# A quarter of the argmax masks as signs and the rows' normalisation on ScalarE, with a new written order

## The chip, the cores and the metric

The kernel runs on one core of a Trainium2 chip. The metric is the device time of one execution in microseconds (us). The engines are TensorE (PE in the profile; PEld is its weight load), VectorE (DVE), ScalarE (ACT), GpSimd (POOL) and SyncE (SP), whose queue issues most transfers.

## What is computed

```python
x  = A_u                                   # 1 x 2048 x 448
xn = layernorm(x)
# A: S4 convolution, N = 256 states per channel
K  = einsum("dn,dnl,dn->dl", C, exp(dt*A*l), dt*B).real      # 448 x 2048
yA = causal_conv(xn, K) + xn * Dskip       # by FFT of length 4096
# B: PEER, 16 heads, 64 x 64 experts, top 1
q  = einsum("nd,dhc->nhc", xn, w_q)        # 2 halves of 256
s1, s2 = q1 @ k1.T, q2 @ k2.T              # 2048 x 16 x 64 each
e  = argmax(s1) * 64 + argmax(s2)
act = gelu(sum(xn * u[e]))                 # per token and head
yB = sum over heads of act * v[e]          # softmax over one entry is 1
out = x + yA + yB
```

## The kernel before, in words

Tokens go in 16 tiles of 128 rows. Four kinds of work run side by side on all engines, and each is cut into steps.

- **Normalisation** (`ln`, two tiles at a time): statistics on DVE (L908, L912), a reciprocal root by three Newton turns on `[128, 2]` tiles (L914 to L919), and the row's normalisation by one DVE instruction per tile (L923), which writes `XN[t][:, 1]`. From it come the transposed tile `xt` (L942, L945), the first transform of the convolution (`u_p`, L723, L726, stored to `vu_d`) and a copy of the rows in memory (`xn_d`).
- **Scores** (`score`, one tile at a time): twelve matmul groups (L960, L969) give four PSUM banks of 8 half-heads x 64 scores, from the ring `s2` of three banks. For each bank DVE takes the maxima (`mx`, L984) and then the mask `eq`, which is 0 where the score is the maximum and 1 elsewhere (L991, `not_equal`). The mask gives the bank back. With all four masks there, DVE subtracts position weights (L999) and takes minima (L1002, L1005), which yields the position of the maximum. Every two tiles the expert numbers are put together (L1021 to L1047) and stored (`ix_st`, L1050).
- **Convolution kernel** (56 batches of 8 channels): exponentials on ACT (L589, L591), phase rows on DVE (L613), sine and cosine on ACT (L628, L631, L634), four products on DVE (L659 to L665, steps `s4_v`), reduction matmuls (L681, `s4_k1`), copies (L689, L692), a transform (L701) and a copy to `VK` (L705, `s4_k4`). After every 16 batches the transform of a chunk of 128 channels is multiplied and transformed back (`cv1` L797, `cv3` L807, `cv5` L829, `cv6` L836), stored (`cv7`, `t_d`), loaded again (`f_l1`, `g_l`) and finished (`f_p`, `g_p` L1176); the last chunk's rows end in L1180 and the store L1188.
- **Experts** (64 groups of 4 gathers): POOL gathers rows of u and v (L1082), DVE makes dot products (`e_d`, L1090), ACT and DVE the gelu (L1097 to L1109), DVE a spread matrix `A` (L1113), PE the weighted sum (`e_p`, L1120), ACT copies it (L1131) and POOL adds it to the output by a transfer.

The order in which steps are written decides the order on every engine's queue. It is a string, `ORDER`: each character names a stream of steps (numbered in the order in which `plan` first adds to them), and the next step of that stream is issued. There is no other scheduler: an engine runs its instructions in the written order and waits on semaphores. Each PSUM bank and buffer ring is given back by a named step. `OPT["SG"]` says how many of a tile's four masks are made by ACT: it is 0 before, and then the branch with `AF.Sign` (L994, L995; eight ACT instructions of 128 x 64) is not used.

Of the kernel before, what the change touches and what calls it, by code (L numbers as in the profile page):

```python
# [172 lines left out]
ORDER = (
    "444447HHHHHHHHHHHHHHHHH4444H4HHHHHHHHHHHHHHHH444MN44444444C7CC676788781222222222222222222211D444D011115EEFCDEFF5CDEFP877"
    "777777II34CDD4EF44444CDCD44379EFEF7J444EKJOWHF6PQPKLCDCDEFJKC8EFD888JEF4444CCDEF4C4K8DDJK4Cuu44EFJKLEFJKDIIPJC9999779777"
    "769777799889D9AALAAAABQQQXXEEFFPQQPQQRRRRRYcccccKMNPPPOPQQQQLWHHHHHHHHHHHHPQQPQQRRRRRRRRRZuZGGGGaZMNPOPWPPbSTTUVvvvQQQQH"
    "HHHHVPQQdeeuPQQRRRRRvdeeMNOWdeeHHHHeeeffJKvvvvvPdPeeQQffJKHHwwHPQPPweeeeccHHHdeQLvHQwxQyxHczeHwwPQwdeezgQRMNHRabzRwxwPcy"
    "x!vvvHHPPRJKzQRcRRzQQPIOWIIIz!vvvwRefRSPHQeefwwxJKQTQyxPwuzTfzQhiabJKXz!LffJKLQRRRfghiRMNPOWPJvvvvveeeeffKJwuwuwxuwyxRzf"
    "ffzKLvghiPHZZdeQzfYH!vvvv#$ghUPQPQQcHHccPwwwxwwyxHQedeeicQHzMNOWjkjkQHzQdeHHRPz!vvvvPPPRRHwRwxwHRHyxRHwzQRHQPHHReedQjzce"
    "eeeRQHz!vvfPQfVvQJwwwueeckjxyxQKJeecQzczcRSTkKLRdeMNOWz!RRedevvvvJfwuwuwxufyxIIcXRPzzz!weeeeePPPTUffffeeVKJKLghQYQQghccc"  # L180
    "HHQwwwxwyxeHHHHPPQcQvvvvvwzcQaZb#$HzHQMNOPWz!vvRiidRPPHwwxwyxHHHVRHHRzzz!eedwHHHIJIQPfRRQPQfKJRRRSffwweedeevvvwuxyTjjTUf"
    "KLghwuvvxzQQePMNOWzz!QQQwuReeeJRPijwuRxyfPxzzz!wffffRHvKJKLweeccvvvvvRvPPeHkkkgd#$cHcQQQPPwwxcVHQQvvfyeedwxzHzHeeQHMNOWd"
    "eeeQPHz!XabHQRwwwxHHHyxZRwPPPRRQzRQQRRhizHz!wRfHjvvvvvvvRQPHIHIHJKwwxPMQyxwzQNOWzSJKLwgefQz!QRwwxPPReefRTTURyxRPzkffegff"
    "fzhidQz!eeQhijkJKffghYuuwuHiePPedVVuvvwwvvvvvvwxwyxHJKLvPQQeedeffjMjHfQQQHNOvP#$ekkzHcHQcHRghdPHcRcHRHzcRz!vvvvHRHRHQeee"
    "eeeeHwwPPHHQQPPMwxweccQRyxwzcedeezQijcQcRRQdNOvwwxz!vvQyxwwuuzJKRPzz!RJSTTURffffVVVVRPQPKLJeeeeeeghIIvK+wuwuwwxRQQfffyxX"
    "PPQJfffiQzfaZbKLPzzQQQwvvkghif!MNORwwvwRjjkkeeexyxRzdPfRRghizPQfPReedezRQRjPQvwvvvwxwyxRSY#!vvvvvvedeQ$zfwwwzTxPPz!vMvve"
    "TQNOvfcQQckyxUVghdPPQczRzVecceeeeeRRezwuwuwuwuPlRQijkRQQ!vvvvcQcffffxyxcPPPllllQzzceedeedeeewQQcXeeez!vvvv#QwwwxRwwwwghm"
    "nmnRRyxRxzRzRz!vvvyxfomnviRwzomllnaZbYzz!vfRomnomnpwwwxwuwufyxffeeefzwughdzzwux$RSoomnmlnccc!TeecyxomomnnTiwzffzdeevvvvv"
    "cqqrzghdeeffff!#pvvoommleeffewiweffeecqqnnewxvvvvghdooUcmyxiczzeedeermccXnnz!vvvYwwwwwxyxzfzdeeewwpoofveewxyxqqzeffezzzm"
    "mlnn!vv!$wuwuoeoccccrjjjkkkghifghjjkkdvvvvwucvewuxyxpffeedijkvzzz!vvvvqfgffffeegaZwwqrhijhibdVV#$+ejewwxwwyxwzzz!vvvvwwe"  # L190
    "eeeffxkdkywwwffgeeefecfccxxzzedhijceedz!v%vvcXyxwuwuzzffzkwueeaZebwuxyYeeefffgd!vvvvxzzhieee&z!v%%vfffff(geedcceedwwwhig"
    "weeejjccc#$xyhijwwwwxzzzkeffkd!vvvveexyxk&ffzzz!vv%vefeefc(gcceedfwwchi&wweedeeaZbjxcYfgewuwukyxzzz(def!vvvvwuwuhijeeeff"
    "kxye&(fffgxzzzefwee!vvvvdcc)v)v)vhijeedeccekwfgdww)vcxyxzzzhijw#!vvvveeffkmmeefewnneomomlnwwwfgfceeedom$ccnomhieedpwwwxy"
    "fcceexXnxyxneeeeqzzz!vvvvwuzzwuz!vYoofaZbfwuqrmmlnonoeeegdeehfffpqwucccccxyxzzzivdeefwmnmn!#$qdeeoowghimnmnlffffgdwweeee"
    "feeefvvvvvvXxomomeedcccwwwwrfpnneedyccXhixzzz!vvvvwxywwwxzzzx!vvvvyeeaZbYoomqqrxzzzefeffnomjghkjjkjkk!vvvvijffgfnopwuwuw"
    "uwueekdfffefhixyeexzzqqrjkffecccghijedewz!%v%edkfgeedww#cchijkwwxyxwwwzzzw!exyeeeffeffgfxzzz!eccccceeedhijvwvvvvvvvweedk"
    "&%(eeafffg&wxyxb$Ywuwuwuwuhijeeee(dezzz!%vvffffffxyv)vkgececceedfhixzzzfeec&(!#vvvv$dewwejwwxywcxzghij)vzz!vkeeefedfkeee"
    "www&(efffXgcccfedvvvchxyxij+cwwYeeffkwdeeeaeebffgdzzz!vvvvwwueehijwuee)v)vkfffgwulccceehijkfwucxyxxcdeedyxffgeeeeXzzz!vv"
    "vvzzwz!vvvvwwhieeejkmeedffffgffcnoeewxcccwmnodecmmlednomnompyxeeYzz#$wwwz!vhiwwweexywnnxzzz!qqreefffghoodvvvvvxyxieffzmm"
    "lnoneeezfofmnzghvmcccciwuwuwuwue!podnxyeeofffqqcvvvvvmnmlnoodeexzghizzwwww!vvveeffeeexwwdwfmmnneecwyxxrpoosleedzmzztml#!"  # L200
    "qqccynefffffxzzzccoedeenojkghieeeffjkjkwww$!slefeeefvvvvvrpqqwxwygffhighiffwsxzzzjkjjkkjkttwwxyxghist!jkzzz!#moommr%pq%q"
    "oomrpqqoo$+*&%()rpqqoorpqqr&%&()&,,,,()()-./-./-.-.//")


class Kernel:
    OPT = dict(UE=8, XX=4, CS=2, ZI=2, MG=4, KT=4, HL=2, SG=0, XR=4, OB=3, XT=1, ST=1)
# [688 lines left out]
    def ln(s, ts):  # L895
        p = s.p
        n = len(ts)
        B = {}
        ld = [s.lnl.get(t) or s.ln_load(t, "ln_ld") for t in ts]

        def st(i, t):
            def f():
                if i == 0:
                    B["mv"] = s.sm.tile([128, n, 2], F32, name="mv", bufs=2)
                    B["bs"] = s.sm.tile([128, n, 6], F32, name="bst", bufs=2)
                    for k in ("v", "y", "q"):
# [8 lines left out]
        ops.append((73, lambda: s.nc.vector.tensor_scalar(B["y"].bitcast(I32), B["v"].bitcast(I32), -0.5, 1597463007.0, op0=ALU.mult, op1=ALU.add)))
        for k in range(3):
            ops.append((73, lambda: s.nc.vector.tensor_mul(B["q"], B["y"], B["y"])))
            ops.append((73, lambda: s.nc.vector.scalar_tensor_tensor(B["q"], B["q"], -0.5, B["v"], op0=ALU.mult, op1=ALU.mult)))
            ops.append((73, lambda: s.nc.vector.scalar_tensor_tensor(B["y"], B["q"], 1.5, B["y"], op0=ALU.add, op1=ALU.mult)))  # L919
        v = p.chain("ln_v", "DVE", ops, deps=[v])  # L920
        for i, t in enumerate(ts):
            def nrm(i=i, t=t):
                s.nc.vector.tensor_scalar(s.XN[t][:, 1], s.XN[t][:, 0], B["mv"][:, i, 0:1], B["y"][:, i:i + 1],  # L923
                                          op0=ALU.subtract, op1=ALU.mult)
# [335 lines left out]
```

## Time and profile before

| | |
|---|---|
| median of 3 runs (lowest, highest) | 822.05 us (821.73, 826.15) |
| profiled execution: its time, its span | 816.38 us, 814.6 us |
| PE busy | 664.8 us (82%) |
| DVE busy | 712.6 us (87%) |
| ACT busy | 512.9 us (63%) |
| POOL busy | 350.1 us (43%) |
| mean granted TensorE clock | 0.907 |
| memory traffic | 212.34 MB, mean 261 GB/s |

The profile is one execution. Its page gives busy times, a strip of the span in 40 slices, the chain of work that ended last, and groups of instructions by line with count, total, mean and the idle time before them. The trace answers by stretch of time, by engine, by line and by wait. An engine's durations overlap a little where instructions follow each other directly, so that a group's busy time can be less than count times mean.

### The profile page before, as it was taken

To read this page: it belongs to the slowest core of one execution; us is meant where nothing else is said; L and a number is where in the kernel's file an instruction comes from. 1 tells how busy PE (TensorE), PEld (TensorE's weight loads), DVE (VectorE), ACT (ScalarE), POOL (GpSimd) and SP (SyncE) were. 2 spreads that over 40 slices of the span, in tenths; PEclk is the share of its full clock that TensorE was granted. 3 is DMA by queue.
4 is the path that set the end of the run, shared out by engine and by line. 5 is a ranking of instruction groups with operands and counts; after the bars stand their busy time and mean duration, and the time that the engine had idled before them with its cause. 6 is when DMAs were issued, how large, how long until landed. Compare 5 with 4: busy or idle time off the path is not lost.

```text
span 814.6 us, 19672 instructions
## 1 busy us (share of the span) xinstructions
PE 664.8 (82%) x7628; PEld 364.7 (45%) x7628; DVE 712.6 (87%) x1751; ACT 512.9 (63%) x931; POOL 350.1 (43%) x303
## 2 busy tenths in 40 slices
PE   1898999899999989999687776767877675688893
PEld 0333334343444334344365553446565343466673
DVE  5697889799999999999989879988898898999940
ACT  0657044646635476465649668987778789887931
POOL 2011042433555433345534645666355657555311
PEclk9999999999999999999989976887979677799997
DMA  9989855785978686687999889989878999889779
GB/s 320 312 317 328 280 180 162 250 258 173 310 219 286 190 259 177 189 249 219 365 313 296 249 270 318 302 289 270 274 222 279 336 290 260 220 249 351 223 181 193
DMA packets 139973, 212.34 MB, mean 261 GB/s; under 512 B 45096, under 2 KB 121896, under 8 KB 139816
## 3 DMA queue, kind: packets, MB, share of 16 engines
q0 software_dynamic: 29120, 124.27, 48.8%
q1 hardware_dynamic: 110760, 86.81, 34.8%
q8 instruction: 60, 0.98, 0.5%
q14 instruction: 33, 0.27, 0.1%
HBM read 181.42 MB, written 33.29 MB: 264 GB/s over the span
## 4 chain that ended last, share of the span: by engine, by line
DVE 33%; PE 31%; ACT 20%; DMA 9%; issue 4%; POOL 1%; SPq 1%; DVEq 0%; ACTq 0%
PE sc L960 8%; DVE ue L1090 7%; DVE ph L613 3%; DMA ue<-in_uv_dram,ig 3%; DVE mg L665 3%; ACT CS L631 3%; PE kp L681 3%; ACT CS L628 3%; PE po L1120 3%; ACT CS L634 3%; DVE zi L661 3%; PE U L797 3%; DVE mx L984 2%; PE ip L829 2%; PE up L723 2%
## 5 line engine op out<-in xcount | busy, mean ns | idle before, releaser
L1082 POOL DMA_INDIRECT ue<-in_uv_dram,ig x256 | 308.6, 1205 | 338.2 <-issue 80.3
L960 PE MATMUL sc<-W,xt 128*128 128x512 f32 x384 | 178.5, 604 | 4.1 <-ACT xt L945 3.5
L1090 DVE SCALAR_TENSOR_TENSOR ue<-ue,xr 128x448 f32<-128x448 f32 x256 | 149.1, 618 | 0.0
L960 PEld LDWEIGHTS sc<-W,xt 128*128 128x128 f32 x384 | 69.4, 190 | 96.1 <-issue 88.5
L681 PE MATMUL kp<-mg 128*32 128x64 f32 x1792 | 65.9, 243 | 31.7 <-DVE mg L665 22.1
L1120 PE MATMUL po<-ue,A 128*32 128x448 f32 x512 | 71.2, 635 | 19.5 <-DVE A L1113 17.8
L589 ACT ACTIVATE mg<-lg 128x512 f32<-128x512 f32 x112 | 61.6, 597 | 20.6 <-PE lg L578 19.9
L681 PEld LDWEIGHTS kp<-mg 128*32 128x32 f32 x1792 | 48.4, 123 | 56.9 <-issue 15.7
L665 DVE TENSOR_TENSOR mg<-mg,CS 128x1024 f32<-128x1024 f32 x56 | 68.1, 1217 | 0.0
L661 DVE TENSOR_TENSOR zi<-mg,CS 128x1024 f32<-128x1024 f32 x56 | 68.1, 1217 | 0.0
L681 PE MATMUL kp<-zi 128*32 128x64 f32 x1792 | 65.4, 240 | 2.8 <-issue 2.8
L628 ACT ACTIVATE CS<-ph 128x1024 f32<-128x1024 int32 x56 | 62.2, 1110 | 6.8 <-DVE ph L613 4.3
L613 DVE CUSTOM_DVE_ANT_0 ph<-st,ph 128x512 uint16<-128x512 uint16 (+2 forms) x84 | 65.1, 775 | 1.2
L634 ACT ACTIVATE CS<-CS,halfpi 128x1024 f32<-128x1024 f32 x56 | 64.3, 1149 | 1.5
L631 ACT ACTIVATE CS<-ph 128x1024 f32<-128x1024 int32 x56 | 62.2, 1111 | 0.0
L578 PE MATMUL lg<-lc,rt 32*128 32x512 f32 x112 | 41.9, 561 | 14.1 <-ACT mg L589 7.1
L797 PE MATMUL U<-VU,g 128*64 128x128 f32 x384 | 44.0, 312 | 11.1 <-ACT tq L836 4.2
L681 PEld LDWEIGHTS kp<-zi 128*32 128x32 f32 x1792 | 50.8, 125 | 0.2 <-issue 0.2
L984 DVE TENSOR_REDUCE mx<-sc 128x8 f32<-128x512 f32 x64 | 43.5, 680 | 7.8 <-PE sc L960 4.2
L829 PE MATMUL ip<-cp,e 64*128 64x256 f32 x384 | 49.0, 410 | 0.0
L701 PE MATMUL vp<-f,kt 128*64 128x128 f32 x448 | 37.3, 299 | 13.8 <-DVE kt L692 12.5
L991 DVE TENSOR_TENSOR eq<-sc,mx 128x512 bf16<-128x512 f32 x64 | 43.6, 682 | 0.7
(244 smaller groups left out, 1184.7 us busy)
## 6 DMA issues: line engine op xcount, KB each, us to landing
wq<-in_wq_dram SPq DMA_DIRECT2D x32, 448.0 KB
xr<-xn_d SPq DMA_DIRECT2D x64, 224.0 KB
vu_d<-vst SPq DMA_DIRECT2D x64, 112.0 KB
VU<-vu_d SPq DMA_DIRECT2D x12, 512.0 KB
t_d<-tq SPq DMA_DIRECT2D x24, 256.0 KB
tl<-t_d SPq DMA_DIRECT2D x12, 512.0 KB
ue<-in_uv_dram,ig POOLq DMA_INDIRECT x256
xx<-in_x_dram SPq DMA_DIRECT2D x16, 224.0 KB
```

What stands on the lines that cost most here:

```text
L613: s.nc.vector.tensor_tensor(out=rw(n, 2 * n), in0=rw(0, n), in1=o["st"][:, k, b0:b0 + 2].rearrange("p b h m x -> p (b h m x)")[:, None].to ...
L628: s.nc.scalar.activation(CS[:, 1].rearrange("p (m r x) -> p m r x", r=16, x=2), four(s.ph), AF.Sin, scale=SC)
L631: s.nc.scalar.activation(B["CS"][:, 0].rearrange("p (m r x) -> p m r x", r=16, x=2), four(s.ph), AF.Abs)
L634: s.nc.scalar.activation(B["CS"][:, 0], B["CS"][:, 0], AF.Sin, scale=-SC, bias=s.halfpi)
L661: V.tensor_tensor(out=zi[:, 512:], in0=mg[:, 512:], in1=CS[:, 1], op=ALU.mult)
L665: V.tensor_tensor(out=mg[:, 512:], in0=mg[:, 512:], in1=CS[:, 0], op=ALU.mult)
L681: s.nc.tensor.matmul(kp[32 * c:32 * c + 32, 64 * gi:64 * gi + 64], T[ri][:, 1024 + m:1056 + m], view(T[ri], m, [[512, 2], [1, 32]]), start ...
L797: s.nc.tensor.matmul(U[64 * h:64 * h + 64, sl, ri], s.g[q][:, 2 * kk + h, ri], src[:, k1 + h, :w], start=True, stop=True)
L960: s.nc.tensor.matmul(B["sc", q].rearrange("p a b -> p (a b)"), B["xt"][:, i], w, start=(q % 2 == 0 and i == 0), stop=(q % 2 == 1 and i == 2))
L1082: s.nc.gpsimd.indirect_dma_start(out=ue, out_offset=None, in_=s.io["uv"], in_offset=bass.IndirectOffsetOnAxis(ap=s.IDX[t][:, c, g:g + 1].b ...
L1090: s.nc.vector.scalar_tensor_tensor(Q["ue", c][:, :D], Q["ue", c][:, :D], 1.0, B["xr", c], op0=ALU.mult, op1=ALU.mult, accum_out=Q["dot"][: ...
L1120: s.nc.tensor.matmul(B["po"][32 * c:32 * c + 32, :D], Q["A"][:, c], Q["ue", c][:, D:], start=(g == 0), stop=(g == 3))
```

## The change

One mask of four (the last bank of each tile) is made by ACT: eight `Sign` activations of 128 x 64, `sign(mx - sc)`, with the maximum as the per-row bias. The row's normalisation is one ACT `Identity` with a per-row scale `y` and bias `q`; `q = -mean * y` is one more DVE instruction on a `[128, 2]` tile per pair of tiles. Both are streams of their own now (`sc_a`, `ln_a`), so that the later streams get other characters, and `ORDER` is written anew throughout.

```diff
-    "444447HHHHHHHHHHHHHHHHH4444H4HHHHHHHHHHHHHHHH444MN44444444C7CC676788781222222222222222222211D444D011115EEFCDEFF5CDEFP877"
...
-    "oomrpqqoo$+*&%()rpqqoorpqqr&%&()&,,,,()()-./-./-.-.//")
+    "04H4HHHHHHHHHHHH4HHHII4744767444H4HHHHHH4444NOHHHHHHHHH678878II444C4444C122222222222222221111DEFCDE4411DEFF444CKDELKF"
...
+    "q*+(osstrqsstq)*+yyyyz!zrsst(####$#$%))./...&-*+/:;/*+/:;:;:;")
...
-    OPT = dict(UE=8, XX=4, CS=2, ZI=2, MG=4, KT=4, HL=2, SG=0, XR=4, OB=3, XT=1, ST=1)
+    OPT = dict(UE=8, XX=4, CS=2, ZI=2, MG=4, KT=4, HL=2, SG=1, XR=4, OB=3, XT=1, ST=1)
...
+        ops.append((73, lambda: s.nc.vector.scalar_tensor_tensor(B["q"], B["mv"][:, :, 0], -1.0, B["y"], op0=ALU.mult, op1=ALU.mult)))
         v = p.chain("ln_v", "DVE", ops, deps=[v])
...
-                s.nc.vector.tensor_scalar(s.XN[t][:, 1], s.XN[t][:, 0], B["mv"][:, i, 0:1], B["y"][:, i:i + 1],
-                                          op0=ALU.subtract, op1=ALU.mult)
-            s.ln_done[t] = p.add("ln_v", "DVE", 425, nrm, deps=[v], give=("lnt",) if i == n - 1 else ())
+                s.nc.scalar.activation(s.XN[t][:, 1], s.XN[t][:, 0], AF.Identity, bias=B["q"][:, i:i + 1], scale=B["y"][:, i:i + 1])
+            s.ln_done[t] = p.add("ln_a", "ACT", ac(D) + 90, nrm, deps=[v], give=("lnt",) if i == n - 1 else ())
```

Read character by character, the two strings differ in what has been written at two places: ahead of the last store of expert numbers (the eighth `ix_st`), and ahead of the copy of the last of the 56 batches (the last `s4_k4`, L705). Streams with the same count are left out.

| steps written ahead of | last `ix_st`: before | after | last `s4_k4`: before | after |
|---|---|---|---|---|
| products `s4_v` (DVE) | 84 | 80 | 224 | 224 |
| phase rows `s4_ph` (DVE) | 56 | 55 | 140 | 140 |
| `cv3` (DVE) | 12 | 8 | 48 | 48 |
| dots `e_d` (DVE) | 116 | 113 | 256 | 250 |
| `e_v2` (DVE) | 84 | 81 | 189 | 186 |
| `s4_lg` (PE) | 34 | 32 | 84 | 84 |
| `s4_k1` (PE) | 20 | 18 | 56 | 56 |
| `cv1` (PE) | 12 | 8 | 48 | 48 |
| `cv5` (PE) | 2 | 1 | 12 | 12 |
| `e_p` (PE) | 28 | 27 | 63 | 62 |
| `s4_act` (ACT) | 143 | 132 | 364 | 364 |
| `cv2`, `cv6` (ACT) | 12, 4 | 8, 0 | 48, 24 | 48, 24 |
| gathers `e_g` (POOL) | 124 | 117 | 256 | 256 |
| `f_l1` (SP) | 0 | 0 | 8 | 10 |

In the new order, DVE has no step between the issue of a tile's signs and its weight subtraction (L999) in tiles 0 and 2, and 2 to 16 steps in the other fourteen. Between a tile's normalisation and its transposes (L942) stand 9 to 61 PE steps of other work, but for tile 0, where there is none. The sequence of ACT's functions changes table set 61 times instead of 63, where `Sign` and `Identity` are counted as in every set.

More of the change, by code (lines that the diff above doesn't have):

```diff
@@ L173 @@
 ORDER = (
-    "444447HHHHHHHHHHHHHHHHH4444H4HHHHHHHHHHHHHHHH444MN44444444C7CC676788781222222222222222222211D444D011115EEFCDEFF5CDEFP877"
-    "777777II34CDD4EF44444CDCD44379EFEF7J444EKJOWHF6PQPKLCDCDEFJKC8EFD888JEF4444CCDEF4C4K8DDJK4Cuu44EFJKLEFJKDIIPJC9999779777"
-    "769777799889D9AALAAAABQQQXXEEFFPQQPQQRRRRRYcccccKMNPPPOPQQQQLWHHHHHHHHHHHHPQQPQQRRRRRRRRRZuZGGGGaZMNPOPWPPbSTTUVvvvQQQQH"
-    "HHHHVPQQdeeuPQQRRRRRvdeeMNOWdeeHHHHeeeffJKvvvvvPdPeeQQffJKHHwwHPQPPweeeeccHHHdeQLvHQwxQyxHczeHwwPQwdeezgQRMNHRabzRwxwPcy"
@@ L178 @@
[L178 to L201, printed above, removed]
@@ L202 @@
-    "oomrpqqoo$+*&%()rpqqoorpqqr&%&()&,,,,()()-./-./-.-.//")
+    "04H4HHHHHHHHHHHH4HHHII4744767444H4HHHHHH4444NOHHHHHHHHH678878II444C4444C122222222222222222221111DEFCDE4411DEFF444CKDELKF"
+    "Q8777777774LC4JJMDEF3CDEFC4K5544444DEF3779999PYH6LKL977M4wC44DCCDD444EFEFQRKL88998777777QEFKL8CKLACDEM899KCJJF44444DEFQC"
+    "677AAADZw889DCDZLM9AABRRRECFDEFaEEFFGGGGQRRewwbQRNOQPYQRSTTTTQQTRRRQRQNOQPYRQQRSTTQTTTTTTTUVVWXxRRQQRceeeeRRRbdNRSTTTTTx"
+    "xxxfggOPYfggxxHHHHHHHHHQHHHHHHHHHHHIIHHHHHHfgggQRKLRygggggQQRRyyyhhz!zHQRKLJJfxxggyyRXe###QRNOPYSQHHHHIIe$eeTgMyyyz!zTQR"
@@ new lines @@
+    "fQxggfgQxxxxe#ggcdTTTRRbb##hhgTTTTURQRycbdQ$xRyyzNOiHRSJJ!zywywxxxVVWXgghh#hhggghT#QQRTTT#QQywTRRRywzyyjk$xxxQKLhR!RQRz#"
+    "##hhZKLPMYSTTTTyXihjkNO$yziQjyKLQxxx!zTThKPYLMHQQRR###HxTyRxayy%&HHhhHz!zHHHHRfggHQR#TTU$xxKLyQefggHHHRRSei#kHHIIJJHK#xT"
+    "Tfgg$xllLKMmmlLKxxyyyzjk!zfTTTLMmVeee###NOPYxVWywQx$xxxQggggggghhRKLywywywzRQeKHQ!zRleggfggHHHR##HmeLM#$eHyQhhijexxxxxyR"
+    "kfggggQNOPYlHyyyhhcHQRQQRSQHhhHHHz!TTggz#H#RT#TyTRQTT%&$yTgggdHHIJIJHhTUxxxyKQRRRVz!zmyyLKLij##MxRRS#VWhhh$xxxNfkiOPYQbT"
@@ new lines @@
+    "TZyyzywTjk!zggTa#KLTQ#hhhRRfggKLMfxlmQlmHHHhXggg#$xxxxijywywRHHeHHeRywzy!zeHeHHH##eggQQRQNRH#$xxRSHhXHHIIJJklmhfOPYKQQgg"
+    "TTTyyLKxyzh!zggggTTTyyT#eh#%&eTTU#yijfgg$xxxLMQReVekyzehH!zRVWKLafg#lKLMRyQ#h#$RhhZgcgghxxxxxgggggdmyyQRRQNRSijfyzhOPYQe"
+    "eeTTeTggf!zeTQRQkggfgggywywywX#T#HRRHQl#$QQywzRHm!zHHHhhggigHh#RHHHHjN##xxxxxRRS$xxHHyyklhTOPhHHIIJJTyyzQTKL%hghggQKLTRi"
+    "TRTee!zyyye##QmfggRRe#Qfgg$TTTUejkxxxxMyzy!zQRfgggaby#KLR#QKLcdVVWl#$xxxxxRShhyNOPQQTmZyzThgggijT!zMThhTywyw#kRQQ#hlywyz"
@@ new lines @@
+    "w!zhigjggRQR#$#hxxxxxxxkRXXRmhh#yQRRfgNOPxlee#$xxxxeyeeSTTmhQgfggyTyzy!zyy&QR##TQfgg#Q%$xxxxTTRRTTyzR!zTUQRQyggi#VRNy#RS"
+    "#yyz$xxxxhhg!OPgTTTz#jkQQhywywywyw##$xxxxz!&VWhhhzlmTTRggeeg#RifggyQQeeefggR##$xxxxQyyyyyXRRRfggQhbjz!zRSannkly##yzT#g%$"
+    "xx&!TyyyymooTznnn##T#$Thpqoz!zghhhppT#cbgijTqoqoXXhxxx#nTTg#$kppiqoZdfghhhgegrj-ywywneqpqggfywywzhUVeeoon!zkeppqqhhhhyxx"
+    "xVWggfgggoposst###pixxxyyggh$iyyyz!%hjkfjkz###$yyrqqoxxxxxgggeeeeeZhhhgggz!z###hhpqxxxfggXXonpq$xxafoosstyygggggg&pphyyr"
@@ new lines @@
+    "qoqolllywywywggeeywz!gepqz###z!mmcbdiimhxxpqz###$xxxjkjksst$yxxxxxfggrsfgglllmmnhhhhiesmfyyyzyhhhjkiglgmeyt!z###jkggyyzy"
+    "lmfX%$x(!zhhggghy&##-hihhgggegfgg#$yyyweejkfgggceeZaz!(ggglmxxxywxhhighhz###$ywywy)gegxxxxhhjkibz!ze*+eee(dfjklglgmmfg##"
+    "#$xxxgfgghhhhiyyyyzf%!z###$gjklghhm)(yxxxxxgghhghhyXgeghh*+xig)gjkf*+geeeeZaigfjkgyygz!zlmlmfyyy)xg###$xxyw*+z!z###$ghhg"
+    "ggggghhigfywywxxxxhhhjkleggfyywz&ggceehi!xxxeez###$xxxxggmyygghhhjkldfyhgghmooiz!z###yyeeepqe%&$xxxgggfyepqggyyopqz!jkop"
@@ new lines @@
+    "qyfgggggghhopopyyhcdhnrqqxz##z!#yyyz##opqopqwwwa$xsstnifghhZbop#gjkoprqqxeeegggfggywzs$xxooxxxhhheepqstfggpqijk!zooyyyyb"
+    "##pprqqhhix#y$xxxxfggggghz!hjksysthhggeopqopqe%&z#hhhylmijkggrsstfgg##$xxxxyyeeeaZz!llmllmmmhfiz###$xggfyyygjklg(zm(gggg"
+    "ggg!zywhhhhihhjeeeefggklmfxywyywwz###$xxxx!z#enn)hhggggggghhcyy#ijkl#$(xgdxxy*+fyhhzmiegeggyyy!z###xjk)fhhhhee%&$(xxx*+x"
+    "lggfggg)*+xeaZghyicmjkl)hgghhgmz!dfhhgez#y*+xi##$ggyygeeejkyy-xxxxfggz!zfggglhhmey###ifgghhyyjkl$xxxxwghhghghbeeemiwwwgh"
@@ new lines @@
+    "ggz!yjkz###fggfggeeZlhiggggayyyyz!chhz##y$xxxx#jklyyggeghd%$xxxmmfhihggfeyyeeez!jklggfyyz##z!#$z#hhhgiyymg#y#$gggghhjklf"
+    "xxxxxxyhhggghmeez!eeez#opqoiggf#pq#ggwywwywopqyyyz!onpqopxyfggghxyxay$opxxxz###z!rqqoonxggghhhiz###pq%ssjkjkg&yyyof$$pqp"
+    "opggggxxhhhhtyersqqsofggoneeeehhpqpqxxz!fggitun&jkhz#gggopi##$ywywhhggggrqoxxxxxvoywhhhhfywssteepqpqjkxxyygghz!unvoneeez"
+    "fgglmlmipfgg###$%xxxxqyyyz!yllmrhijklz###uggg&hhghsstghhjkigg$xx((hhjklmlmhiyyz!z###ujklmyy$vvxxxmmooqqrqqo,)yyz!z#sstrq"
```

## The prediction

> **What bounds the kernel now.** I read the page first: its busy times and the chain by engine.
>
> ```profile
> span 814.6 us, 19672 instructions
> PE 664.8 (82%) x7628; PEld 364.7 (45%) x7628; DVE 712.6 (87%) x1751; ACT 512.9 (63%) x931; POOL 350.1 (43%) x303
> DVE 33%; PE 31%; ACT 20%; DMA 9%; issue 4%; POOL 1%; SPq 1%; DVEq 0%; ACTq 0%
> ```
>
> DVE is the fullest engine, but only a third of the chain that ended last is its own; PE has nearly as much. An average over the span hides that there are stages. So next came the busy time by stretch, cut at three places: 50, 395 and 780 us, and again at 429.5 us, where the last expert numbers are made, and 780 us, where the last of the 56 batches is copied. The two rows after the stretches give these places.
>
> ```profile
> 0.00:50.00 50.00, 29.73 (x121) 12.55 (x121) 34.13 (x65) 18.32 (x43) 6.84 (x18) 1.00 0.96 329
> 50.00:395.00 345.00, 323.95 (x2148) 137.48 (x2148) 321.81 (x806) 184.33 (x328) 128.69 (x111) 0.99 0.75 236
> 0.00:429.50 429.50, 378.58 (x2612) 167.50 (x2614) 386.77 (x958) 222.33 (x409) 151.37 (x143) 0.98 0.79 255
> 429.50:780.00 350.50, 264.69 (x4573) 179.66 (x4568) 319.16 (x783) 284.87 (x509) 192.63 (x156) 0.83 0.89 274
> 780.00:814.60 34.60, 21.57 (x452) 17.55 (x448) 6.65 (x12) 5.67 (x13) 6.11 (x5) 0.84 0.93 189
> L1047 DVE SCALAR_TENSOR_TENSOR ix<-exg,rcg x8: 173/188/192, 104.9 to 429.3; 128x32 f32<-128x32 f32 x8
> L705 ACT ACTIVATE VK<-vp x56: 356/383/418, 182.2 to 779.5; 128x256 f32<-128x256 f32 x56
> ```
>
> Columns are stretch, length, then PE, PEld, DVE, ACT, POOL busy, the granted clock, the DMA share and GB/s. In the first 50 us the transfers bind (share 0.96). While scores are made (50 to 395 us), PE is busy 324 of 345 us and DVE 322: they bind together, with ACT at 53%. After 429.5 us DVE is busy 91%, ACT 81%, PE 76% at a clock of 0.83: DVE binds, with ACT close. In the last 34.6 us DVE does almost nothing: the chain is matmul, copy, store, load, matmul. Last I read who waited, in the first stretch and the tail.
>
> ```profile
> PE po L1120 <- DVE A L1113: 6.8, 6, 2.3
> DVE mx L984 <- PE sc L960: 4.2, 2, 2.4
> DVE mx L984 <- PE sc L969: 3.6, 3, 3.0
> DVE bb L1180 <- PE po L1176: 20.6, 4, 18.7
> ```
>
> Both ways of waiting are there during the scores: PE for DVE and DVE for PE. That is what two co-bound engines look like, and it is the reason why I don't pass on DVE's whole saving.
>
> **What is removed and added.** The rows (line, engine, operation, count | busy us, mean ns):
>
> ```profile
> L991 DVE TENSOR_TENSOR eq<-sc,mx 128x512 bf16<-128x512 f32 x64 | 43.6, 682 | 0.7
> L923 DVE TENSOR_SCALAR xx<-xx,mv,y 128x448 f32<-128x448 f32 x16 | 7.8, 529 | 0.1
> L918 DVE SCALAR_TENSOR_TENSOR q<-q,v 128x2 f32<-128x2 f32 x24 | 3.9, 164 | 0.3
> L689 ACT ACTIVATE kt<-kp 128x126 f32<-128x126 f32 x56 | 15.3, 276 | 17.1 <-PE kp L681 16.9
> L631 ACT ACTIVATE CS<-ph 128x1024 f32<-128x1024 int32 x56 | 62.2, 1111 | 0.0
> L634 ACT ACTIVATE CS<-CS,halfpi 128x1024 f32<-128x1024 f32 x56 | 64.3, 1149 | 1.5
> L1131 ACT ACTIVATE ob<-po 128x448 f32<-128x448 f32 x16 | 8.7, 541 | 2.8 <-PE po L1120 2.8
> L638 ACT ACT_TABLE_LOAD x28 | 35.9, 1283 | 0.4
> L589 ACT ACT_TABLE_LOAD x25 | 32.1, 1283 | 0.4
> ```
>
> DVE loses a quarter of the masks, 43.6/4 = 10.9 us, and 7.8 us of normalisation; eight small instructions like L918 come in, 8 x 0.16 = 1.3 us. Net -17.4 us, all of it before 395 us.
>
> ACT has no `Sign` row. The nearest is the 128x126 copy out of PSUM, 276 ns; against the 541 ns of 448 columns an element costs (541 - 276)/322 = 0.82 ns, so 64 columns take 276 - 51 = 225 ns. A bias read per row adds some 38 ns, by the sine with `halfpi` against the plain one (1149 - 1111). Upper end 263 ns each; lower end 125 ns, if they overlap by the 0.10 us that these two rows show, where the second starts 0.28 us into a 0.38 us copy:
>
> ```profile
> 78.17 0.38 ACT L880 ACTIVATE W<-wt__666 128x256 f32<-128x256 f32 x1
> 78.45 0.27 ACT L881 ACTIVATE W<-wt__666 128x128 f32<-128x128 f32 x1
> ```
>
> I take the upper end, for short instructions on one bank: 8 x 0.263 = 2.1 us a tile in place of 0.68, and 34 us in all (lower end 16). `Identity` on 448 columns is the 541 ns copy plus about 38 for its bias: 16 x 0.58 = 9.3 us. ACT gains 25 to 43 us, nearly all ahead of 429.5 us, where it idles 429.5 - 222.3 = 207 us. Two fewer table changes give back 2 x 1.28 = 2.6 us. I cost ACT's load at nothing; the cover is that idle time. What could bring it back is not load but lateness, in the third rival.
>
> The normalisation's new place costs nothing either: 9 to 61 PE steps stand between it and the transposes in every tile but the first, and while PE works through them ACT has time to come to it. In the first tile the path is longer by one small DVE instruction and the difference of the two rows, 0.16 + 0.05 = 0.2 us, in a stretch that waits for transfers. What queues behind the identity on ACT is the next copy or exponential, later by 0.58 us; the store of the rows on SP (`xn_st`) starts as much later, and its readers, the experts, come two tiles behind.
>
> The head is reordered as well: the constants' memsets on POOL come first, the constants' loads earlier among the 45 loads of weights and rows. The bytes are the same and the first 50 us are bound by them (share 0.96), so I cost this at nothing; if a load that PE needs slipped behind another of its size, 448 KB at 329 GB/s, it would be 1.4 us either way.
>
> **What is moved.** The table of steps written ahead of two places splits the span in three stages. Rows needed beyond those above:
>
> ```profile
> L659 DVE SCALAR_TENSOR_TENSOR zi<-mg,CS 128x512 f32<-128x512 f32 x56 | 38.3, 685 | 4.7 <-ACT CS L628 4.4
> L661 DVE TENSOR_TENSOR zi<-mg,CS 128x1024 f32<-128x1024 f32 x56 | 68.1, 1217 | 0.0
> L807 DVE TENSOR_TENSOR cp<-us,U 128x512 f32<-128x512 f32 x48 | 31.2, 679 | 3.7 <-ACT us L802 1.7 <-ACT kt L689 1.1 <-PE po L1120 0.9
> L1113 DVE TENSOR_TENSOR A<-mask,th 128x128 f32<-128x128 f32 x64 | 18.4, 288 | 1.2
> L1106 DVE SCALAR_TENSOR_TENSOR th<-th,dot 128x4 f32<-128x4 f32 x64 | 10.0, 156 | 9.1 <-ACT th L1103 8.2 <-issue 0.8
> L802 ACT ACTIVATE us<-U 128x256 f32<-128x256 f32 x48 | 17.6, 385 | 16.8 <-PE U L797 16.6
> L836 ACT ACTIVATE tq<-ip 128x512 f32<-128x512 f32 (+1 forms) x32 | 16.1, 545 | 10.7 <-PE ip L824 7.2 <-issue 2.9 <-PE po L1120 0.5
> 723.09 1.64 DVE ue L1090 x6
> 741.22 1.90 PE U L797 x32
> 796.95 6.03 DMA hl<-in_h_dram
> 737.14 3.65 PE ip L829 x32
> 479.83 1.27 PE kp L681 x64
> 746.99 0.50 PE L578 MATMUL lg<-lc,rt 32*128 32x512 f32 x2
> 755.57 1.10 PE L578 MATMUL lg<-lc,rt 32*128 32x512 f32 x2
> 762.65 0.96 PE L1120 MATMUL po<-ue,A 128*32 128x448 f32 x8
> ```
>
> Stage 1, to the last expert numbers (429.5 us). DVE: -17.4 removed, and moved behind: one batch's four products 2 x (0.69 + 1.22) = 3.8, four `cv3` 4 x 0.68 = 2.7, three dots 1.6 (six rows are three dots and their readouts), small steps about 1. Together -26.5. PE, all of it moved behind: four `cv1` 2 x 1.90 = 3.8, one `cv5` 3.65, two `s4_k1` 2 x 1.27 = 2.5, two `s4_lg` at 0.50 to 1.10, 1.5 as an estimate, one `e_p` 0.96: -12.4. With them go one store of a transformed quarter (`cv7`, two transfers), one load of `VU` and seven gathers; they leave a stage whose DMA share is 0.79, and I cost them at nothing there. If DVE sets the pace the stage loses 26.5 us, if PE does, 12.4. The chain gives them equal parts (33 to 31%), so I take the middle: -19.
>
> Stage 2, to the copy of the last batch. What was moved behind arrives: DVE +9.1, PE +12.4, and ACT eleven steps `s4_act`, between a plain copy's 0.55 and a sine's 1.15 us each, four `cv2` (0.39) and four `cv6` (0.55), 10 to 16, say 13. Out of it, into the tail, go six dots (3.3), two steps `e_v1` and one group's three `e_v2` (four instructions like L1106 and one L1113, 0.9): DVE's net is +5. DVE binds there; ACT's 13 on 285 of 350 us and PE's 12 on 265 have room, but not everywhere. Ends: +5 (DVE alone) and +12 (whatever PE and ACT get, the stage gets). I take +6, next to DVE's end, since DVE has the least room. The seven gathers and the load arrive here too, where the DMA share is 0.89 already. POOL's own queue is busy 193 of 350 us, so it can issue them; whether they land in time is the part of the +12 end that I can't see in the old trace.
>
> Stage 3, the tail. Those 4 us of DVE work fall into its wait of 18.7 us, but two weighted sums (0.96 us each) instead of one now stand on PE ahead of the last finish, and the output's last accumulation and its reading back come later. On the other side two loads of the third chunk leave the tail's queue. Ends -1 and +6, by the loads' issue (two of some 0.5 us) and by one transfer as long as the tail's load of 6.03 us more on its chain; I take +2, next to the weighted sums, as the accumulation has other finishes beside it.
>
> Sum: -19 + 6 + 2 = -11, between -26.5 + 5 - 1 = -22.5 and -12.4 + 12 + 6 = +5.6. The profiled execution took 816.38 us (its span and 1.8 us around it) and would take 805.4. It lies 5.7 us below the median of the three runs; from that median, 822.05 - 11 = **811 us**.
>
> **The rivals.**
>
> *All of DVE's saving comes through.* If PE can be kept fed in stage 1, the lower ends hold: 822 - 22.5 = 799.5 to 805 us. For it: the order is written anew for these durations, and DVE is 91% busy after the scores. Against it: PE at 324 of 345 us.
>
> *PE holds, and the change does next to nothing.* Stage 1 loses only the PE work that was moved out (12.4), and stage 2 takes it back (+12): 822 us, between 818 and 826. For it: the waits of DVE on score matmuls, and that PE's total work is unchanged.
>
> *Slower: the signs come late on DVE's own path.* The weight subtraction (L999) needs all four masks, and every later DVE step queues behind it. Before, the last mask was DVE's own, 0.68 us. Now DVE waits for ACT's 2.1 us, plus whatever ACT has in front: a table change and a trio of sine steps are 1.28 + 1.15 + 1.11 + 1.15 = 4.7 us. The bank is also given back later, and `s2` has three. Nothing covers this in tiles 0 and 2; 2 to 16 steps do in the others. The point from which it decides: a mean lateness of 11/16 = 0.7 us a tile beyond the cover eats the forecast gain; at 1.7 us it costs 16 more: 827 us, up to 835. The Trainium skill (ScalarE: Activation LUTs, Rules for kernel authors) speaks for this one: simple arithmetic belongs on VectorE, not ScalarE. The rows agree on the price (2.1 us against 0.68), but say too that ACT idles half of this stage.
>
> *`Sign` needs a table load.* In the trace ACT alternates between two sets, with 28 loads ahead of the sines (L638) and 25 ahead of the exponentials (L589). If `Sign` were in neither set, each tile's signs would bring up to two more loads, 16 x 2 x 1.28 = 41 us of ACT; half of them stand ahead of the signs, 20.5 us on the path of the third rival: 811 + 20 = 831 us. The same page of the Trainium skill (Table sets: the hidden batching unit) names copy, identity and abs as members of every set, and not Sign. `Square`, which it does not name there either, has no load at its line L1097 in this trace, which is why I hold this unlikely.
>
> **How the numbers follow.** Forecast (805 to 818 us) 0.46; all of the saving (799 to 805) 0.17; PE holds (818 to 826) 0.19; late signs (826 to 835) 0.14; table loads 0.04. About 0.5% (4 us) is what a measurement here tells from no change, so below 818 is faster: 0.46 + 0.17 = 0.63. Same is 0.19, slower 0.18. The range leaves out a little of the first rival and most of the last two: 799 to 827.
>
> **What the next profile would show.** Right: 48 DVE masks of about 682 ns, 128 ACT signs of 0.13 to 0.27 us, 16 identities near 0.58, DVE busy near 695 us, some 61 table loads; the last expert numbers near 410 us; stage 2 about 6 us longer; DVE waiting for signs below 5 us in all. Wrong: the last expert numbers later than 417 (PE holds), DVE waits for signs above 10 us (late signs), 80 or more table loads, or a tail above 40 us.

## The result, and the profile after

The changed kernel takes 813.14 us (median of 4 runs, 810.53 to 815.05) against 823.52 us before (821.73 to 826.15, 4 runs): ratio 0.9897, 95% interval [0.9848, 0.9947]: a gain of about 1%, clear of no change. A ratio leaves out runs more than 1.5% above the fastest of their kernel, so that it can differ from the quotient of the medians, which are of all runs. The profiled execution took 810.53 us with a span of 808.8 us, 5.8 us less than the profiled execution before, which was a quick one for its kernel; this pair of profiles shows about half of the 10.4 us between the medians. The forecast was 811 us.

From the page after, busy times and the chain by engine:

```profile
span 808.8 us, 19792 instructions
PE 662.6 (82%) x7628; PEld 360.9 (45%) x7628; DVE 701.3 (87%) x1727; ACT 539.9 (67%) x1069; POOL 346.4 (43%) x303
DVE 42%; PE 25%; ACT 19%; DMA 7%; issue 4%; SPq 1%; POOL 0%; DVEq 0%; ACTq 0%; POOLq 0%
```

DVE has 11.3 us less on the page and ACT 27 us more. The span fell by half of what DVE lost; DVE's idle time went up from 102.0 to 107.5 us. PE's share of the chain fell, DVE's rose: DVE is still the fullest engine. The groups that changed (line, engine, operation, count | busy us, mean ns | idle before):

```profile
L991 DVE TENSOR_TENSOR eq<-sc,mx 128x512 bf16<-128x512 f32 x48 | 32.9, 685 | 2.2 <-PE po L1120 1.5
L999 DVE TENSOR_TENSOR eq<-eq,wt 128x2048 bf16<-128x2048 bf16 x16 | 19.6, 1223 | 4.8 <-ACT eq L995 4.5
L920 DVE SCALAR_TENSOR_TENSOR q<-mv,y 128x2 f32<-128x2 f32 x8 | 1.3, 161 | 0.3
L995 ACT ACTIVATE eq<-sc,mx 128x64 bf16<-128x64 f32 x128 | 27.9, 335 | 2.4 <-DVE mx L984 1.2 <-DMA ue<-in_uv_dram,ig 0.5 <-ACT mg L589 0.4
L924 ACT ACTIVATE xx<-xx,q,y 128x448 f32<-128x448 f32 x16 | 11.4, 774 | 9.2 <-DVE q L920 9.2
```

The 128 signs last 335 ns each but fill only 27.9 us, 0.22 us apiece, because they overlap; eight of them run in 1.74 us. The weight subtraction (L999) waited 4.5 us for them in all. No table load stands at L995 or, after the first, at L924.

For the stages, one date has to be put right first. The table in the section on the change counts steps *written ahead of* the last `ix_st`. The prediction dated that place by L1047, the last arithmetic on the expert numbers. In the old order 25 DVE steps are written between L1047 and the store, in the new order none. By the counts of the table, the place in the old order is where DVE has finished 116 dots and 12 `cv3`. The trace before, around it:

```profile
441.46 1.21 DVE L665 TENSOR_TENSOR mg<-mg,CS 128x1024 f32<-128x1024 f32 x1
...
442.81 0.61 DVE L1090 SCALAR_TENSOR_TENSOR ue<-ue,xr 128x448 f32<-128x448 f32 x1
...
443.35 1.27 DVE L807 TENSOR_TENSOR cp<-us,U 128x512 f32<-128x512 f32 x2
```

The dot at 442.81 is the 116th, and the two `cv3` behind it end at 444.6 us: stage 1 was 444.6 us long, not 429.5. After, the place does fall on L1047:

```profile
L1047 DVE SCALAR_TENSOR_TENSOR ix<-exg,rcg x8: 183/184/193, 106.9 to 430.4; 128x32 f32<-128x32 f32 x8
L705 ACT ACTIVATE VK<-vp x56: 356/383/442, 196.9 to 770.3; 128x256 f32<-128x256 f32 x56
```

| stage | before | after | difference | forecast |
|---|---|---|---|---|
| 1, to the place of the last `ix_st` | 444.6 | 430.5 | -14.1 | -19 |
| 2, to the last batch's copy | 334.9 | 339.8 | +4.9 | +6 |
| 3, the tail | 35.1 | 38.5 | +3.4 | +2 |
| sum | 814.6 | 808.8 | -5.8 | -11 |

Busy times by these stages (columns as before): first stage 1 before, up to its corrected place, then the three stages after.

```profile
0.00:444.60 444.60, 390.84 (x2856) 176.87 (x2856) 401.87 (x987) 236.34 (x433) 158.59 (x149) 0.98 0.80 257
0.00:430.50 430.50, 381.34 (x2702) 168.48 (x2702) 381.13 (x942) 255.64 (x558) 152.45 (x145) 0.98 0.79 258
430.50:770.50 340.00, 257.54 (x4458) 174.64 (x4462) 308.84 (x754) 277.78 (x495) 186.88 (x152) 0.81 0.91 274
770.50:808.80 38.30, 23.76 (x472) 17.80 (x464) 11.35 (x34) 6.44 (x18) 7.08 (x6) 0.78 1.02 213
```

In stage 1 PE and DVE are busy 381 us each, of 430.5: still bound together. DVE lost 20.7 us of work there, PE 9.5, and the stage lost 14.1, between the two.

In the tail DVE has 11.4 us of work instead of 6.7, as the moved dots lead one to expect, but only 1% of the tail's chain is DVE's. Three transfers stand on it, where one load of 6.03 us stood before:

```profile
770.79 6.78 DMA hl<-in_h_dram
787.99 4.26 DMA t_d<-tq
792.79 6.81 DMA tl<-t_d
```

One execution doesn't fix the later stages. In the changed kernel's profile of the first set below, the two places come at 431.2 and 763.1 us of a span of 804.7: against the profile before, stage 1 loses 13.4 us, stage 2 loses 3.0 and the tail gains 6.5. Only stage 1's figure repeats.

### The profile page after: what moved, and what is told of

Its sections match the earlier page's. It is cut to its first block, busy times and chain, and to the rows that moved or that the text cites. A ratio compares the mean times of both kernels' runs of the same rounds, so it can differ in the third digit from the quotient of the medians.

```text
span 808.8 us, 19792 instructions
## 1 busy us (share of the span) xinstructions
PE 662.6 (82%) x7628; PEld 360.9 (45%) x7628; DVE 701.3 (87%) x1727; ACT 539.9 (67%) x1069; POOL 346.4 (43%) x303
## 4 chain that ended last, share of the span: by engine, by line
DVE 42%; PE 25%; ACT 19%; DMA 7%; issue 4%; SPq 1%; POOL 0%; DVEq 0%; ACTq 0%; POOLq 0%
DVE ue L1090 8%; PE sc L960 8%; DVE mg L665 4%; DVE ph L613 3%; DVE mx L984 3%; ACT CS L631 3%; DVE zi L661 3%; DMA t_d<-tq 2%; ACT CS L634 2%; PE po L1120 2%; ACT CS L628 2%; DMA hl<-in_h_dram 2%; DVE eq L991 2%; PE U L797 2%; ACT L638 2%
## 5 line engine op out<-in xcount | busy, mean ns | idle before, releaser
L1082 POOL DMA_INDIRECT ue<-in_uv_dram,ig x256 | 303.9, 1187 | 323.4 <-PE po L1120 101.4
L960 PE MATMUL sc<-W,xt 128*128 128x512 f32 x384 | 182.5, 616 | 10.1 <-ACT xt L945 9.3
L960 PEld LDWEIGHTS sc<-W,xt 128*128 128x128 f32 x384 | 70.8, 193 | 100.0 <-issue 85.1
L681 PE MATMUL kp<-mg 128*32 128x64 f32 x1792 | 65.1, 240 | 36.4 <-DVE mg L665 16.3
L681 PEld LDWEIGHTS kp<-mg 128*32 128x32 f32 x1792 | 47.5, 121 | 59.7 <-issue 21.2
L681 PE MATMUL kp<-zi 128*32 128x64 f32 x1792 | 64.8, 238 | 0.2 <-issue 0.2
L701 PE MATMUL vp<-f,kt 128*64 128x128 f32 x448 | 39.2, 309 | 20.3 <-DVE kt L692 18.4
L681 PEld LDWEIGHTS kp<-zi 128*32 128x32 f32 x1792 | 49.7, 123 | 0.9 <-issue 0.7
L797 PE MATMUL U<-VU,g 128*64 128x128 f32 x384 | 42.1, 300 | 6.9 <-DVE cp L807 4.8
L1097 ACT ACTIVATE x<-dot 128x4 f32<-128x4 f32 x64 | 13.2, 206 | 49.7 <-DVE ue L1090 44.5
L701 PEld LDWEIGHTS vp<-f,kt 128*64 128x64 f32 x448 | 26.6, 150 | 43.4 <-DVE kt L692 23.7
```

The costliest lines, as they stand in the source:

```text
L681: s.nc.tensor.matmul(kp[32 * c:32 * c + 32, 64 * gi:64 * gi + 64], T[ri][:, 1024 + m:1056 + m], view(T[ri], m, [[512, 2], [1, 32]]), start ...
L960: s.nc.tensor.matmul(B["sc", q].rearrange("p a b -> p (a b)"), B["xt"][:, i], w, start=(q % 2 == 0 and i == 0), stop=(q % 2 == 1 and i == 2))
L1082: s.nc.gpsimd.indirect_dma_start(out=ue, out_offset=None, in_=s.io["uv"], in_offset=bass.IndirectOffsetOnAxis(ap=s.IDX[t][:, c, g:g + 1].b ...
```

## The experiments

Three sets of runs were made, each with runs of the kernel before on the same chip; all ratios are to that kernel within the set.

**First set** (the kernel before: 822.45 us, 17 runs). It separates the engines' part from the order's.

*The changed kernel itself.*

> The changed kernel itself, timed beside the others so that each can be set against it on one chip. Every theory expects a ratio near 0.99 to the kernel before, 0.985 to 0.995.

810.13 us, ratio 0.9856 [0.9808, 0.9904].

*The new order with both operations on DVE.*

```diff
-        ops.append((73, lambda: s.nc.vector.scalar_tensor_tensor(B["q"], ...)))
+        ops.append((73, lambda: None))
-                s.nc.scalar.activation(s.XN[t][:, 1], s.XN[t][:, 0], AF.Identity, ...)
+                s.nc.vector.tensor_scalar(s.XN[t][:, 1], s.XN[t][:, 0], B["mv"][:, i, 0:1], B["y"][:, i:i + 1],
+                                          op0=ALU.subtract, op1=ALU.mult)
-                if q not in sign:
+                if True:
```

> The new written order, but the fourth mask and the normalisation are DVE's again, in the same places of the order. My theory (DVE's 11 to 17 us less work is what gains; the order only spreads it): the gain goes, ratio to the kernel before 1.00 to 1.01, DVE busy some 11 us above the changed kernel's 701. Rival (the new order itself is better, whoever does the work): ratio stays at 0.985 to 0.993. A second rival (order and engines fit only together): above 1.01.

819.16 us, ratio 0.9946 [0.9910, 0.9982]. So the new order alone gives 3.3 us, and the two operations' move to ACT in that order 9.0 more. Single runs spread over 17 us for this kernel and over 9 for the changed one, so both figures are good to a few microseconds. The pages' busy rows, this kernel's first, then the changed kernel's of the same set:

```profile
PE 661.3 (81%) x7628; PEld 361.9 (44%) x7628; DVE 718.0 (88%) x1751; ACT 503.9 (62%) x925; POOL 353.6 (43%) x303
```

```profile
PE 655.1 (81%) x7628; PEld 357.3 (44%) x7628; DVE 701.7 (87%) x1727; ACT 539.1 (67%) x1069; POOL 348.8 (43%) x303
```

DVE has 16.3 us less for 9.0 us of time: about half came through. In these two profiles, with the same written order, L1047's instruction and L705's copy can be set side by side (its line number is L1048 here):

```profile
L1048 DVE SCALAR_TENSOR_TENSOR ix<-exg,rcg x8: 184/186/193, 104.2 to 436.5; 128x32 f32<-128x32 f32 x8
L705 ACT ACTIVATE VK<-vp x56: 362/384/408, 197.9 to 771.2; 128x256 f32<-128x256 f32 x56
```

```profile
L1047 DVE SCALAR_TENSOR_TENSOR ix<-exg,rcg x8: 178/186/192, 108.6 to 431.2; 128x32 f32<-128x32 f32 x8
L705 ACT ACTIVATE VK<-vp x56: 363/383/442, 198.5 to 763.1; 128x256 f32<-128x256 f32 x56
```

All of the work that DVE lost lies ahead of the first row, yet the place comes only 5.3 us earlier. Stage 1 of the two, with columns as before:

```profile
0.00:436.50 436.50, 382.81 (x2702) 169.56 (x2702) 398.29 (x964) 219.70 (x414) 157.13 (x145) 0.98 0.79 254
0.00:431.20 431.20, 382.24 (x2702) 169.53 (x2702) 381.87 (x942) 255.34 (x558) 155.62 (x145) 0.98 0.80 257
```

DVE is busy 16.4 us less, PE as long as before, and DVE's idle time there goes up by 11.1 us. 2.8 us more come in stage 2 and 1.1 in the tail, where DVE's work is the same in both; what shortens these is not shown. Among the waits that grew beside the scores are DVE's for signs, 0 to 4.5 us, and PE's for the transposed tile `xt`, which ACT copies, 6.3 to 8.9 us:

```profile
PE sc L961 <- ACT xt L946: 6.3, 8, 1.9
```

```profile
DVE eq L999 <- ACT eq L995: 4.5, 3, 2.2
PE sc L960 <- ACT xt L945: 8.9, 9, 2.2
```

Together 7.1 us, the size of what did not come through (16.3 - 9.0 = 7.3). That the sizes agree is no proof, as waits of two engines need not add, and others moved too: in stage 1 DVE's wait for PE's scores rose from 11.3 to 12.8 us and its wait for a parameter that ACT makes (L434) from 4.6 to 7.6.

*The old order with both operations on ACT.* The signs and the identity stand where DVE's instructions stood; `q` is issued within the last Newton step.

```diff
-    OPT = dict(..., SG=0, ...)
+    OPT = dict(..., SG=1, ...)
-                x1 = p.add("sc_a", "ACT", ...)
+                x1 = p.add("sc_v", "ACT", ...)
-                s.nc.vector.tensor_scalar(s.XN[t][:, 1], ...)
+                s.nc.scalar.activation(s.XN[t][:, 1], s.XN[t][:, 0], AF.Identity, bias=B["q"][:, i:i + 1], scale=B["y"][:, i:i + 1])
```

> The old written order, with the fourth mask as signs and the normalisation on ACT, in the places where DVE did them. My theory: part of the gain comes, since the old order has little DVE work between masks and weight subtraction: 16 waits of 1 to 2 us, 16 to 32 us, against 17 saved: ratio 0.995 to 1.01, DVE waiting for signs 10 to 30 us. Rival (the engines alone make the gain, order is noise): 0.985 to 0.992. Rival (the order makes the gain): 1.00 without any sign waits.

871.67 us, ratio 1.0594 [1.0544, 1.0645]: 49 us slower, outside every expectation. The waits of this kernel that the one before does not have (L929 is the identity, L1000 the signs, L1004 the weight subtraction):

```profile
DVE eq L1004 <- ACT eq L1000: 39.3, 14, 5.7
ACT xx L929 <- DVE q L924: 28.6, 5, 11.8
ACT eq L1000 <- DVE mx L989: 25.4, 4, 16.1
PE xtp L947 <- ACT xx L929: 17.6, 1, 17.6
```

DVE waits for signs in 14 of 16 tiles, and ACT, which runs its queue in order, stands 54 us in front of identities and signs whose inputs DVE has not made yet, with everything behind them waiting too. The prediction's rival of late signs is real in these places, and the new order keeps it away. Whether DVE's wait or ACT's queue costs the 49 us, this run alone doesn't say; the last experiment bears on it.

*Every Sign issued twice.*

```diff
-                for j in range(8 * q, 8 * q + 8):
+                for j in [*range(8 * q, 8 * q + 8)] * 2:
```

> The changed kernel with every Sign issued twice (the second writes the same values): ACT gets 28 us more in the stage of the scores. My theory (ACT has room there and the signs are mostly covered): 0 to 8 us more, ratio to the kernel before 0.990 to 1.000, DVE's waits for signs rise from 4.5 to at most 15 us. Rival (late signs set the pace): 16 to 28 us more, ratio 1.01 to 1.025.

836.17 us, ratio 1.0128 [1.0069, 1.0187]: 26.0 us more than the changed kernel, for 26.3 us of ACT time (565.4 against 539.1). My expectation fell, the rival's 16 to 28 us held. The two waits from above, in this kernel:

```profile
DVE eq L999 <- ACT eq L995: 21.2, 12, 3.8
PE sc L960 <- ACT xt L945: 16.1, 11, 3.8
```

They grew by 16.7 and 7.2 us. Three of the six runs took 829 to 832 us and three 840 to 844, the profiled one among them, so the 26.0 us stand for 20 to 32. ACT is idle 41% of stage 1 in the changed kernel and still has little room there: most of a second burst of 1.7 us a tile goes to the end.

**Second and third set** (the kernel before: 860.14 us, 17 runs, and 865.53 us, 11 runs). The kernel before itself took some 5% longer here than in the first set, and the changed kernel 7.6% longer; what differs in the profiles is in the last section. Ratios hold within a set only, and the expectations of the second set were made for the first set's conditions, so that the variants of the new order all lie above them. That is why the changed kernel and its variants were run together once more.

*The changed kernel again.*

> The changed kernel again. In the last set the kernel before itself took 860 us where it had taken 822, and PE's reduction matmuls and weight loads were slower in every profile, so the ratios of that set can only be read against a changed kernel in the same set. If the kernel before takes about 822 us here: ratio 0.985 to 0.99. If it takes about 860: 1.00 to 1.02, should the changed kernel be as sensitive to that state as its three variants were.

871.32 us, ratio 1.0197 [1.0126, 1.0268] in the third set. The kernel before varied from 851 to 872 us here, and the medians, 871.32 and 865.53, are only 0.7% apart. Under these conditions the change makes the kernel slower, by some 1 to 2%; whether by as much as 2% is not resolved.

*Masks back on DVE, normalisation on ACT.*

```diff
-                if q not in sign:
+                if True:
```

> The changed kernel with the fourth mask made by DVE again, in its place of the new order; the normalisation stays on ACT. Issuing each Sign twice cost 26 us for 28 us of ACT time, so a first theory now says that ACT's time among the scores is not free: then taking the signs away gains nearly as much as DVE's 10.7 us cost, ratio to the kernel before 0.980 to 0.992 (as the changed kernel or better). Second theory (one burst of signs is covered by the order, the second stands out): the gain of the signs is lost, ratio 0.993 to 1.00, DVE busy 711.

> The changed kernel with the fourth mask by DVE. Against the changed kernel of this set. Theory (signs pay): 4 to 9 us more, DVE busy 10 us more. Rival (ACT's 28 us cost as much as DVE's 10.7 us gain, as the doubled signs suggest): within 3 us.

Ratio 1.0163 [1.0111, 1.0215] in the second set and 1.0224 [1.0153, 1.0294] in the third, 875.82 us: 4.5 us above the changed kernel, with overlapping intervals, so that theory and rival are not told apart.

*Normalisation back on DVE, signs on ACT.* The edit is the first two parts (`q` and the normalisation) of the one in the first set that puts both operations back.

> The changed kernel with the normalisation by DVE again, in the places of the new order; the signs stay on ACT. If both parts pay in proportion to the DVE time they free (7.8 of 18.5 us), ratio 0.988 to 0.993, between the changed kernel (0.986 to 0.990) and the new order with both on DVE (0.995). If the normalisation on ACT is what gains, 0.995; if it costs (ACT 11.4 us, and PE's first transposes wait for it), 0.980 to 0.985.

> The changed kernel with the normalisation by DVE. Against the changed kernel of this set. Theory (it pays by DVE's 7.8 us): 3 to 7 us more. Rival (the identity's 11.4 us and its place ahead of PE's transposes cost as much): within 3 us, or less time.

Ratio 1.0103 [1.0060, 1.0145] and 1.0144 [1.0068, 1.0220], 868.46 us: 2.9 us below the changed kernel, where the rival had it. Which of the two parts pays is not resolved by these differences, and the sets say nothing on it for the conditions of the first.

*All signs covered.* In the changed kernel's order, each first weight subtraction is moved behind at least five DVE steps; 119 of 3421 characters differ.

> The changed kernel with at least five DVE steps between a tile's signs and its weight subtraction also in the five or six tiles that had fewer (0 to 3). DVE waited 4.5 us for signs there. Theory (these waits lie on the path): 3 to 6 us less than the changed kernel, ratio to the kernel before 0.980 to 0.985. Rival (PE or ACT take the time, the wait moves): no change beyond 2 us.

> The changed kernel with at least five DVE steps between signs and weight subtraction in every tile. Against the changed kernel of this set. Theory (DVE's 4.5 us of sign waits are on the path): 3 to 6 us less. Rival (the wait moves): within 2 us; or more, if later expert numbers make the gathers late.

Ratio 1.0193 [1.0133, 1.0254] and 1.0251 [1.0180, 1.0321], 878.44 us in the third set: 7 us above the changed kernel, not below. The wait did go, from the changed kernel's row of this set to this one's:

```profile
DVE eq L999 <- ACT eq L995: 4.4, 3, 2.2
```

```profile
DVE eq L999 <- ACT eq L995: 1.3, 2, 1.0
```

Taking these waits away did not give their time back here. The first expert numbers (L1047) come 17.4 us later, at 124.9 us instead of 107.5, as the rival has it; that this makes the 7 us is not shown.

*The old order, both on ACT, signs covered by six DVE steps.* 217 of 3413 characters differ.

> The old written order with both parts on ACT (which took 872 us), where only the first weight subtraction of each tile is moved behind six DVE steps of other work (0 to 4 before), with what depends on it. Theory (the new order was needed to cover the signs): DVE's waits for signs fall from 39 us to below 10, and the time by 20 to 40 us, ratio to the kernel before 1.01 to 1.035. Rival (what costs is that ACT's queue stands behind signs and identities that wait for DVE, not DVE's own wait): waits fall, time by less than 12 us, ratio 1.045 to 1.06.

Ratio 1.0598 [1.0534, 1.0663] in the second set, where it was 1.0594 without the cover in the first. The waits of this kernel:

```profile
DVE eq L1004 <- ACT eq L1000: 8.5, 4, 5.1
ACT xx L929 <- DVE q L924: 26.4, 5, 11.4
ACT eq L1000 <- DVE mx L989: 24.8, 5, 15.4
```

DVE's waits for signs fell from 39.3 to 8.5 us, ACT's waits in front of identities and signs stayed at 51 us, and the time did not move. The theory fell, the rival held: what costs in the old order is most likely not DVE's wait but the place of the new steps in ACT's queue, ahead of their inputs. As the two kernels ran under different conditions, this is shown for the waits and only likely for the time.

## Why the prediction was right, point by point

- **The time.** 811 us forecast, 813.14 measured, on the forecast's side of 0.5%. In the profiled pair stage 1 gained 14.1 us instead of 19, and the other two gave back 8.3 instead of 8; in the first set's profile of the same kernel they gave back 3.5. The profiled pair lost 5.8 us in all and the medians 10.4, so the number came nearer than the stages can bear out.
- **Half of DVE's saving.** The central choice, taking the middle between DVE's end and PE's, is borne out in size. The forecast's own sum splits into -8.7 us for the removal (the middle of -17.4 and 0) and -2.8 for the order (the middle of -9.1 and -12.4, then +6 and +2); the first set has -9.0 and -3.3, with a few microseconds of doubt on each. In stage 1 the ends themselves were too wide, 20.7 us for DVE and 9.5 for PE instead of 26.5 and 12.4, and the 14.1 us lie near their middle. The reason is shown in part: PE stays busy 382 us in stage 1 whoever makes the masks. Besides PE's co-bound, the loss has the size of waits on ACT (signs, `xt`), and the runs don't divide it between the two.
- **The tail.** It was to grow by 2 us for weighted sums on PE. It grew by 3.4 and 6.5 in two profiles, the second of them above the 40 us named as a sign of being wrong (41.6), and in the profile after no weighted sum stands on its chain. Transfers do, which the prediction had only at its upper end. That the size is near is luck.
- **Where the place was dated.** L1047 was taken for the place of the last `ix_st`. In the old order the place is 15.1 us later. This did not enter the sum, which used counts, but the check "last expert numbers near 410 us" failed by it: they come at 430.4 us. The sign of being wrong, later than 417, is off by the same 15.1 us; put at 432.1, it is just not met.
- **ACT's load at nothing.** This term was not nothing. The first 39 us of ACT work came with some 7 us of DVE's saving lost, of which ACT's part is not known; the next 26 us cost 20 to 32. Idle share was the wrong measure of room; among the waits that grew are those in which DVE and PE stand for ACT.
- **A sign's price.** 263 ns taken, 335 measured for one, but 218 in a row; a burst is 1.74 us, 2.1 forecast. The identity was 0.58 us by a plain copy plus one operand; 774 ns measured. The Trainium skill (ScalarE: Activation LUTs, What ACT_TABLE_LOAD costs) gives 280 ns and 0.833 per element where the bias is a per-row operand, an estimate of 333 ns for a sign of 64 columns, which the 335 measured bear out. By the Trainium skill's figures in the same section for two such operands, the estimate for the identity is 745 ns, against 774 measured.
- **Late signs.** 4.5 us of waits, below the 5 that were named. The count of covering steps, though, was wrong: tiles 0, 1, 2, 5 and 13 have no DVE step between signs and subtraction, not 0 and 2; tile 12 has three and the others five to eleven. Three tiles waited.
- **Table loads.** No load is put ahead of `Sign`. Loads of all kinds fell from 68 to 62, by six and not by two.
- **DVE busy** was to be 695 us and is 701. The removal did take what was summed: 16.3 us in one order, against the 17.4. But the new order with both operations on DVE shows 718.0 us where the old shows 712.6, with the same 1751 instructions. The order adds 5.4 us of DVE's busy time, which the prediction had at nothing.

## What to carry to other kernels

A busy engine's relief is worth its work only where nothing else binds beside it: here about half of it arrived. Moving an instruction to an idle engine means placing it in that engine's queue behind its inputs: the same two operations gained 9 us in an order written for them and cost 49 us in the places where they had stood. An idle share does not measure room; doubling the moved work comes nearer to it.

## What the runs showed of the hardware that was not expected

The same changed kernel took 810 us in the first set and 871 us in the third, and the kernel before 822 and 866. The profile of the changed kernel in the third set, its chain by engine and by line:

```profile
PE 46%; ACT 21%; DVE 18%; issue 6%; DMA 5%; another core or an unknown queue 2%; SPq 1%; POOL 0%; ACTq 0%; DVEq 0%; POOLq 0%
PE sc L960 17%; PE kp L681 6%; PE po L1120 4%; ACT CS L631 3%; PE sc L969 3%; PE U L797 3%; DVE ue L1090 3%; ACT CS L628 3%; ACT CS L634 3%; PE lg L578 2%; PE vp L701 2%; ACT L638 2%; PE up L723 2%; PE ip L829 2%
```

In the first set DVE had 41% of the chain and PE 26%. PE's rows that changed most are its gaps ahead of the small matmuls of L681, for which the profile shows no releaser: first the third set, then the first.

```profile
PEld kp L681 <- issue: 68.9, 110, 4.8
PE kp L681 <- issue: 31.6, 75, 1.8
```

```profile
PEld kp L681 <- issue: 23.7, 36, 4.8
```

Weight loads waited 110 times instead of 36, and matmuls 75 times where there was no such row before; the durations of single matmuls are the same (219 ns median at L681 in both), and the mean of a score matmul (L960) is 632 ns against 618, at a granted clock of 0.883 against 0.912. So PE was hardly slower at its work but began it late, most of all where the instructions are dense and small. DVE's wait for the copies of what L681 makes (L692) grew with it, from 4.7 to 41.1 us. What causes it was not found: the runs change nothing outside the kernel. The first and second sets are on record for the same chip, the third for another, so the chip alone doesn't decide it. The kernel before was not profiled in these sets. What follows is therefore argued and not shown: when PE is held up in this way it is the bound, DVE's relief buys little, and the order that was written for the other balance costs time. That is the rival "PE holds" and more, and it limits the verdict: faster by 1.0 to 1.4% in the first runs, where DVE has the largest share of the chain, slower by some 1 to 2% in the third set, where PE has.
